# A new cost table for a kernel's instruction planner, with 36 instead of 100 products of zeros, in an attention block's forward and backward pass

## The chip, the cores and the metric

One core of a Trainium2 chip runs the whole program. Its engines work at the same time, each through its own list in order: PE multiplies matrices, DVE, ACT and POOL compute element by element, and SP's list here issues nearly all the DMA copies. The metric is the time of one execution in microseconds (us). A run of the profiler is one more execution; its span is what lies between its first and its last instruction.

## The reference

The block is a Branchformer layer on x of shape (2, 4000, 144): one branch is attention over all 4000 tokens, the other a gated unit with a convolution of five taps; both are merged by a second convolution and a matrix. What is computed is the output and, by `jax.vjp`, the gradients of x and of seven weights, in bfloat16.

```python
xa = _layernorm(x, axis=-1)
qkv = jnp.einsum('btd,de->bte', xa, w_qkv)
scores = jnp.einsum('btd,bsd->bts', q, k) * D ** (-0.5)
p = _softmax(scores, axis=-1)
attn = jnp.einsum('bts,bsd->btd', p, v)
glob = jnp.einsum('btd,de->bte', attn, w_att_out)
h = _gelu(jnp.einsum('btd,de->bte', xc, w_mlp_in))
...
loc = jnp.einsum('btd,de->bte', u * gc, w_mlp_out)
m = jnp.concatenate([glob, loc], axis=-1)
...
return x + jnp.einsum('btc,cd->btd', m, w_merge)
```
```python
_out, _vjp = jax.vjp(_f, x, w_qkv, w_att_out, w_mlp_in, dw_csgu, w_mlp_out, dw_merge, w_merge)
_grads = _vjp(grad_out)
```

## The kernel before

**Tiles.** A batch of 4000 tokens is 32 blocks of 125. The attention of one block of queries is one step; with two batches there are 64 steps, numbered through. In step s, four rounds of products fill PSUM tiles `ps` (L1276 with 128 rows, L1283 with the remaining 16): the scores of block s against 1000 keys, and beside them the gradient products of block s - 1. DVE copies the scores to `Pbuf` and takes their minimum (`S_min`, L1298), ACT makes the exponentials in place (L1304), and SP turns the two halves of `Pbuf` into `PT` by DMA transposes (L1308). PE then forms Y (`yz` from `PT`, L1325, 32 products in two halves). The gradient products go to `Sbuf` (ACT L1314 and DVE L1316, or DVE alone L1312), are transposed to `ST` (L1492) and give Z (L1363, 32 products). The products X (L1410) add the gradient of the keys' side; DVE sums them in `acc` (L1414, L1416). All Y and Z share one PSUM buffer of the pool `ps_yz`; X, `pt`, `pj`, `pd` and others share three of `ps_w`.

**Stages.** The head (steps 0 and 1) loads weights and tokens, normalises the tokens (statistics L380 and following, normalised blocks `xa_aug` by DVE L403, ACT L401 and POOL L405), transposes them (`pt`, L410 and L414), copies the result to `xaT_m` and `R` (L411, L415), and makes combined weights (`hps`) between the first scores. The first token tile is loaded by two copies, L42 (112 rows) and L43 (13 rows); so are the three others, and the gradient `go_q`. Beside the attention, in each batch, the gated branch runs in small units (`ph`, `pd`, `pc`, `pw`). At the change of batch (steps 26 to 38) the second batch's tokens and gradients (`xa_aug`, `pgo_h`, `gq`) are loaded, and the sums of the first are stored (`acc_d`). After step 63 a merge (`Hps`, `po`, `pm`, `pz`) and the weights' gradients end the program.

**Products of zeros.** The head also issues `WARM` products of a zero tile `wz` (L187), whose output `warm` is a tile of `ps_yz` that nobody reads.

**Order.** The program is first recorded in source order. `Planner.plan` then groups PE's products, works out which group needs which, and goes through modelled time: each engine, when free, takes the ready group with the smallest key. A key is the place in the source plus a number of `LEAD`, so a negative entry lets a kind of instruction go early and a positive one holds it back; zero products have the largest key, and fill gaps. An entry's name is stage, engine, output tile and size, for some tiles also which one of a step. No group may run further ahead than a window allows. `cost` gives an instruction's length and the time until its result can be used. The resulting order is fixed in each engine's list, whatever the true times are. Copies on SP's list also wait for the copy eight places ahead, since they use eight completion semaphores in turn.

Of the kernel before, what the change touches and what calls it, by code (L numbers as in the profile page):

```python
# [16 lines left out]
DR = 16  # L17
# [523 lines left out]
WARM = 100  # L541
# [247 lines left out]
class Planner:  # L789
# [101 lines left out]
    def cost(self, e, ins):  # L891
# [5 lines left out]
        if "Dma" in kind or "DMA" in kind:  # L897
            if kind == "InstDmaTransposeAnt":
                return (1.8, 4.3) if n > 1500 else (1.2, 3.0)
            return 0.5, 2.2  # L900
# [4 lines left out]
        f32 = any(a.bass_ap.tensor.dtype == F32 for a in aps_i[:1] + aps_o[:1])  # L905
        if e == "DVE":
            if kind in ("InstTensorTensor", "InstTensorCopy") and not psum and not f32:
                d = 0.155 + n / 1920.0
            elif kind == "InstTensorScalarPtr" and not psum and not f32 and len(aps_i) == 1:
                d = 0.22 + n / 3800.0  # L910
            elif kind == "InstBNStats":
                d = 0.3
            else:
                d = 0.155 + n / 960.0
            acc = len(aps_o) > 1
            if acc and n < 300:
                d += 0.14
            return d - 0.05 + (0.07 if acc else 0), d + (0.14 if acc else 0.06)
        if e == "Activation":
            d = 0.17 + n * (0.00096 if kind == "InstActivation" and not psum else 0.00084)  # L920
            return d - 0.08, d + 0.06
        d = {"InstTensorCopy": 0.24 + n / 1250.0, "InstTensorTensor": 0.16 + n / 480.0}.get(kind, 0.36 + n / 1700.0)
        if kind == "InstTensorTensor" and n <= 8:
            d = 0.43 + 0.15 * n
        return d, d + 0.06

    def plan(self, i0, i1, window=400, late=1 << 40, early=0):
# [111 lines left out]
        for a, b in self.pairs:  # L1039
            if a in gof and b in gof and gof[a] != gof[b]:  # L1040
                after[gof[a]].add(gof[b])

        for g in groups:
            d, end = 0.0, 0.0
            if g["e"] == "PE" and g["sg"]:
                m = [i for i in g["ins"] if i.ins[0].bass_ap.ap[0][1] >= 128]
                if len(m) < len(g["ins"]):
                    d = len(m) * 0.21 + 0.094 + 0.22 + 0.16
                    end = d - 0.14 + 0.22
# [3 lines left out]
            else:  # L1053
# [4 lines left out]
                if g["e"] == "PE":  # L1058
                    d, end = d + 0.02, end + 0.02
# [29 lines left out]
        for g, G in enumerate(groups):  # L1089
            if any(n.startswith("nm_") for _, n in allocs[g]):  # L1090
                turn = {}
# [1156 lines left out]
```

## Time and profile before

| what | us |
|---|---|
| median of 3 runs | 1287.58 (1287.13 to 1288.39) |
| the profiled execution | 1292.98 |
| its span | 1291.2 |
| PE busy in the span | 1257.1 |
| DVE busy | 1047.1 |
| ACT busy | 788.2 |
| POOL busy | 501.1 |
| mean granted clock of TensorE | 0.991 of full |

Busy time is the union of an engine's instructions. PE's products overlap each other, and the end of one is modelled, so PE can be shown as busy without a pause and yet stream fewer columns than it could. The matmul rows give the mean duration of one product (229 ns for 144 columns), not the spacing at which they follow each other (62 to 63 ns). 16 DMA engines moved 185.80 MB in 628829 packets, 604215 of them under 512 bytes; the queue of SP, ACT and the transposes (q1) took 76.7% of their time.

### The profile page before, as it was taken

Reading aid. Unit: us, or ns where it says so; the run is one execution under the profiler, and the core shown is the slowest. Engines: PE = TensorE matmul, PEld = TensorE weight load, DVE = VectorE, ACT = ScalarE, POOL = GpSimd, SP = SyncE. Lnnn points to the kernel's source line nnn. Section 1 sums busy time; section 2 is a strip of 40 time slices with the busy share of each in tenths; the row PEclk is TensorE's granted clock in tenths of the full one; section 3 lists DMA queues with packets and bytes.
Section 4 is the critical chain, followed back from the end, with each engine's and each line's share of the span. In section 5 each row is a group of like instructions: output and inputs, shape, how many; then the busy total and the mean of one; then the engine's idle time right before and its main releaser. Section 6 shows DMA issues by size and latency. Waiting matters only on the chain.

```text
span 1291.2 us, 39494 instructions
## 1 busy us (share of the span) xinstructions
PE 1257.1 (97%) x15974; PEld 1040.6 (81%) x15974; DVE 1047.1 (81%) x2809; ACT 788.2 (61%) x1291; POOL 501.1 (39%) x976
## 2 busy tenths in 40 slices
PE   8999999999999999899899999999999999899898
PEld 6578888888888887777678888888888888799897
DVE  6589888988888887898888888899889887666925
ACT  4776666666665666556656666667566665435561
POOL 6265335444443434232444434444443433132410
PEclk8899999999999999999999999999999999999999
DMA  4477888888888888889898898887778788959611
GB/s 126 94 141 136 155 144 152 143 145 150 137 151 142 145 143 162 158 145 174 168 155 148 133 149 135 151 137 146 137 142 154 136 155 167 188 123 208 186 44 50
DMA packets 628829, 185.80 MB, mean 144 GB/s; under 512 B 604215, under 2 KB 623065, under 8 KB 628625
## 3 DMA queue, kind: packets, MB, share of 16 engines
q1 hardware_dynamic: 627506, 181.88, 76.7%
q8 instruction: 125, 2.05, 0.6%
q0 software_dynamic: 592, 1.18, 0.3%
q14 instruction: 58, 0.48, 0.1%
q10 hardware_dynamic: 548, 0.21, 0.1%
HBM read 22.96 MB, written 16.69 MB: 31 GB/s over the span
## 4 chain that ended last, share of the span: by engine, by line
PE 83%; DMA 6%; DVE 3%; ACT 3%; SPq 2%; POOL 1%; issue 1%; ACTq 0%; POOLq 0%
PE X L1410 20%; PE ps L1276 15%; PE yz L1363 10%; PE yz L1325 9%; PE ps L1283 7%; DMA ST<-Sbuf 2%; PE po L1783 2%; DMA PT<-Pbuf 2%; PE pd L625 1%; PE pd L692 1%; PE pc L677 1%; PE pj L1249 1%; PE Hps L1698 1%; PE pt L1265 1%; PE pw L737 1%; DVE Pbuf L1298 1%
## 5 line engine op out<-in xcount | busy, mean ns | idle before, releaser
L1298 DVE TENSOR_SCALAR_CACHE_REDUCE Pbuf<-ps 125x1000 bf16<-125x1000 f32 x256 | 306.4, 1197 | 93.9 <-PE ps L1283 90.0
L1304 ACT ACTIVATE Pbuf<-Pbuf,nm 125x1000 bf16<-125x1000 bf16 x256 | 278.6, 1130 | 91.1 <-DVE nm L1300 90.7
L1410 PE MATMUL X<-QBs,Sbuf 125*125 125x144 bf16 x2048 | 298.8, 229 | 0.8 <-DVE acc L1414 0.4
L1410 PE MATMUL X<-QBs,Pbuf 125*125 125x144 bf16 x2048 | 292.3, 226 | 0.0
L1410 PEld LDWEIGHTS <-Sbuf 125*125 125x125 bf16 x2048 | 259.3, 137 | 26.0 <-issue 25.8
L1314 ACT CAST Sbuf<-ps 125x1000 bf16<-125x1000 f32 x190 | 188.7, 993 | 132.4 <-PE ps L1283 131.1
L1276 PE MATMUL ps<-xaT_m,qt 128*125 128x500 bf16 x1024 | 263.7, 378 | 2.9 <-DVE Pbuf L1298 2.1
L1410 PEld LDWEIGHTS <-Pbuf 125*125 125x125 bf16 x2048 | 260.6, 137 | 0.9 <-issue 0.9
L1416 DVE TENSOR_TENSOR acc<-X,acc 125x432 f32<-125x432 f32 (+1 forms) x373 | 200.5, 549 | 25.2 <-PE X L1410 22.3
L1363 PE MATMUL yz<-xa_aug,ST 125*125 125x144 bf16 x2048 | 150.6, 228 | 6.1 <-DMA ST<-Sbuf 4.8
L1276 PEld LDWEIGHTS <-qt 128*125 128x125 bf16 x1024 | 121.5, 137 | 42.8 <-issue 4.6
L1325 PE MATMUL yz<-xa_aug,PT 125*125 125x145 bf16 x2048 | 146.1, 228 | 6.5 <-DMA PT<-Pbuf 6.5
L1363 PEld LDWEIGHTS <-ST 125*125 125x125 bf16 x2048 | 139.4, 138 | 9.9 <-DMA ST<-Sbuf 6.1
L1325 PEld LDWEIGHTS <-PT 125*125 125x125 bf16 x2048 | 137.4, 137 | 9.6 <-DMA PT<-Pbuf 7.4
L1316 DVE TENSOR_TENSOR Sbuf<-Sbuf,Pbuf 125x1024 bf16<-125x1024 bf16 x190 | 134.6, 710 | 3.5 <-ACT Sbuf L1314 3.1
L1283 PEld LDWEIGHTS <-qt 16*125 16x125 bf16 x1024 | 36.6, 128 | 101.2 <-issue 101.2
L1283 PE MATMUL ps<-XR,qt 16*125 16x500 bf16 x1016 | 111.1, 420 | 0.0
L1343 POOL TENSOR_SCALAR QBs<-qb,rl 125x144 bf16<-125x144 bf16 x64 | 27.0, 422 | 180.5 <-DVE rl L1331 151.1
L1312 DVE TENSOR_TENSOR Sbuf<-ps,Pbuf 125x1000 bf16<-125x1000 f32 x66 | 78.8, 1194 | 6.7 <-PE ps L1283 6.2
L720 POOL TENSOR_TENSOR A_dwc<-l_fl,A_dwc 128x512 f32<-128x512 f32 (+2 forms) x48 | 37.0, 771 | 78.8 <-ACT l_fl L719 78.8
L1267 ACT COPY qt<-pt 128x500 bf16<-128x500 bf16 x62 | 35.9, 578 | 45.5 <-PE pt L1265 44.8
L595 POOL TENSOR_SCALAR l_a<-l_sq 125x576 bf16<-125x576 bf16 x32 | 22.5, 702 | 101.6 <-ACT l_sq L593 101.3
(576 smaller groups left out, 2411.3 us busy)
## 6 DMA issues: line engine op xcount, KB each, us to landing
Yn_d<-yn SPq DMA_DIRECT2D x64, 35.2 KB
Zn_d<-zn SPq DMA_DIRECT2D x64, 35.2 KB
ug_d<-ugr SPq DMA_DIRECT2D x32, 70.3 KB
PT<-Pbuf SPq DMA_TRANSPOSE x126
ST<-Sbuf SPq DMA_TRANSPOSE x126
Yg<-Yn_d SPq DMA_DIRECT2D x8, 252.0 KB
go_h<-in_grad_out_dram SPq DMA_DIRECT2D x8, 252.0 KB
Yg<-ug_d SPq DMA_DIRECT2D x8, 252.0 KB
```

The lines of the kernel that those rows point to most:

```text
L720: nc.gpsimd.tensor_tensor(acc, fl[0:rows, 0:n], acc, op=ALU.add)
L1276: mm = nc.tensor.matmul(pp[r // 2][:, r % 2, 0:CH], QT[i][:, 3 * h, :], bs(i)[0].xaT_m[:, c * CH:(c + 1) * CH], start=True, stop=False)
L1283: nc.tensor.matmul(pp[r // 2][:, r % 2, 0:CH], QT[i][rs, 1 + (q // 2 + h) % 2, :], xr, start=False, stop=True)
L1298: nc.vector.tensor_scalar(pv(Pbuf, i % NPB, c2), src, -1.0, 3.0e38, op0=ALU.mult, op1=ALU.min, accum_out=NM[i][:, c2:c2 + 1])
L1304: nc.scalar.activation(v, v, ACT.Exp, bias=NM[i][:, 4:5], scale=-1.0)
L1312: nc.vector.tensor_tensor(pv(Sbuf, i % NDB, c2), src, pv(Pbuf, i % NPB, c2), op=ALU.mult)
L1314: nc.scalar.copy(pv(Sbuf, i % NDB, c2), src)
L1316: nc.vector.tensor_tensor(sc, sc, pchunk(i % NPB, c2), op=ALU.mult)
L1325: nc.tensor.matmul(Y, PT[0:PB, j, 0:PB], S.xa_aug[:, j, 0:D + 1], start=(j == 0), stop=(j == NB - 1))
L1363: nc.tensor.matmul(Z, ST[0:PB, j, 0:PB], S.xa_aug[:, j, 0:D], start=(j == 0), stop=(j == NB - 1))
L1410: nc.tensor.matmul(X[:, jj, :], l, r, start=(n_ == 0), stop=(n_ == len(ops) - 1))
L1416: nc.vector.tensor_tensor(av, X[:, 0:nj, :], av, op=ALU.add)
```

## The change

The planner's model is altered in five ways, and its table of leads is new. The instructions that compute the result stay the same; their order in every list changes.

- `cost` has other lengths for DVE, ACT and POOL instructions, by kind, size and operands.
- DMA copies and transposes get a function `moved` and a model of the transfer queue: a transpose begins when the copies ahead have landed, and SP's list is held until then.
- The time from an instruction's end to its waiter depends on the waiter's engine (`wait`).
- `LEAD` has entries for two further stages, "B" (steps 26 to 38) and "E" (from step 60 on).
- `WARM` falls from 100 to 36, and a zero product may only be placed after the first group of `pt` has been (`lead`); its modelled length is doubled.

In the new order the first zero products stand behind the transposes of the first token tile, and the last four of them directly ahead of the first Y.

```diff
-WARM = 100
+WARM = 36
...
     LEAD = {
-        "H DVE raw 1008": -246, "H POOL ident 128": 38, "H POOL Wi 288": 113, "H POOL xa_aug 32": 32, "H POOL go_q 576": -13, "H SP go_q 576": -144,
...
+        "H SP go_q 1152": -233, "H SP go_q 288": -318, "H POOL qr 256": -26, "H DVE lnst 6": 16, "H DVE xa_aug 144": 105, "H ACT goT 250": 186,
...
+        "B SP pgo_h 288": -381, "B SP xa_aug 1152": 4, "B SP gq 576": -211, "B DVE pst 6": 72, "B SP acc_d 432": 145,
...
-                d = 0.155 + n / 960.0
-            acc = len(aps_o) > 1
...
+                d = 0.067 + n / 960.0
+            d += 0.06 * (one > 0) + 0.025 * (one > 1)
+            return d, d + 0.083
...
+    def moved(self, ins):
+
+        a = ins.outs[0]
+        n = self.count(a)
+        if type(ins).__name__ == "InstDmaTransposeAnt":
+            return (2 if n > 1500 else 3), n / 2048.0
+        b = n * (4.0 if a.bass_ap.tensor.dtype == F32 else 2.0) * a.bass_ap.ap[0][1]
+        src = next((q for q in ins.ins if hasattr(q, "bass_ap")), None)
+        far = src is not None and getattr(src.bass_ap.tensor, "tag_meta", None) is None
+        return (1 if far else 0), b / 200e3
...
+        lead = next(g for g, G in enumerate(groups) if G["e"] == "PE" and G["t"].startswith("pt"))
+        for g, G in enumerate(groups):
+            if G["x"] < 0:
+                after[g].add(lead)
...
-            c = "%s %s %s %d" % ("T" if G["x"] >= late else "H" if G["x"] < early else "A", E[G["e"]], t, 0 if G["e"] == "PE" else self.count(a))
+            c = "%s %s %s %d" % ("T" if G["x"] >= late else "H" if G["x"] < early else "B" if 26 <= step < 39 else "E" if step >= 60 else "A", E[G["e"]], t, 0 if G["e"] == "PE" else self.count(a))
...
+        wait = {"PE": 0.053, "DVE": 0.034, "Activation": 0.034, "Pool": 0.09, "SP": 0.055}
...
-                        if kind == "InstDmaTransposeAnt":
-                            n = 0.1 + n * 2.65 / 2000
...
-                        dmq = max(s + 0.2, dmq) + n
-                        end = max(s + G["d"], dmq + 2.1)
+                        how, v = self.moved(G["ins"][0])
+                        if how == 2:
+                            q = max(s + 1.83, dmq + 0.15)
+                            d, end = q - s + 0.05, q + 2.6
+                        elif how == 3:
+                            d, end = 1.25, max(s + 2.4 + 1.3 * v, dmq + 2.4 * v)
                         else:
-                            n *= (4.0 if a.bass_ap.tensor.dtype == F32 else 2.0) * a.bass_ap.ap[0][1] / 220e3
+                            end = max(s + (2.2 if how else 1.55) + v, dmq + v)
+                        dmq = max(dmq, end)
```

More of the change, by code (lines that the diff above doesn't have):

```diff
@@ L897, in cost @@
         if "Dma" in kind or "DMA" in kind:
-            if kind == "InstDmaTransposeAnt":
-                return (1.8, 4.3) if n > 1500 else (1.2, 3.0)
             return 0.5, 2.2
@@ L905, in cost @@
         f32 = any(a.bass_ap.tensor.dtype == F32 for a in aps_i[:1] + aps_o[:1])
+        one = sum(n > 8 and self.count(a) == 1 for a in aps_i[1:])
+        memset = "Memset" in kind or not aps_i
         if e == "DVE":
[L907 to L910, printed above, removed]
+            if memset:
+                d = 0.07 + n / (1000.0 if f32 else 2500.0)
+            elif kind == "InstTensorReduce":
+                d = 0.067 + n / 960.0
@@ L923, in cost @@
-        if kind == "InstTensorTensor" and n <= 8:
-            d = 0.43 + 0.15 * n
-        return d, d + 0.06
+                d = 0.21
+            elif n <= 8:
+                d = 0.08
+            elif kind in ("InstTensorTensor", "InstTensorCopy") and not f32 and (not psum or len(aps_i) == 1):
+                d = 0.067 + n / 1900.0
+                if psum and aps_o[0].bass_ap.ap[0][1] == DR:
+                    d += 0.12
+            elif kind == "InstTensorScalarPtr" and not psum and not f32:
+                d = 0.067 + n / 1920.0
+            else:
+                d = 0.067 + n / 960.0
@@ new lines, in cost @@
+            d += 0.06 * (one > 0) + 0.025 * (one > 1)
+            return d, d + 0.083
+        if e == "Activation":
+            d = 0.054 + n * 0.000821 + 0.09 * (one > 0) + 0.135 * (one > 1)
+            if not psum and one < 2 and kind == "InstActivation":
+                d += 0.046
+            return d, d + 0.108
+        if memset:
+            d = 0.04 + n / 1150.0
+        elif kind == "InstTensorCopy":
+            d = 0.105 + n / 1150.0
+        elif kind == "InstTensorTensor":
+            d = 0.43 + 0.15 * n if n <= 8 else 0.16 + n / 480.0
+        else:
+            d = 0.36 + n / 1700.0
@@ L1048, in plan @@
                     d = len(m) * 0.21 + 0.094 + 0.22 + 0.16
-                    end = d - 0.14 + 0.22
+                    end = d + 0.06
                 else:
@@ L1058, in plan @@
                 if g["e"] == "PE":
-                    d, end = d + 0.02, end + 0.02
+                    d += 0.023
+                    if g["x"] < 0:
+                        d *= 2.0
             g["d"], g["end"] = d, end
@@ L1087, in plan @@
         tagof = {n: t for al in allocs for t, n in al}
-        key, turn = [], {}
+        key, turn, step = [], {}, 0
         for g, G in enumerate(groups):
@@ L1091, in plan @@
                 turn = {}
+                step += 1
             a = G["ins"][0].outs[0]
             t = re.sub(r"\d*(_\d+)?$", "", a.bass_ap.tensor.name)
-            c = "%s %s %s %d" % ("T" if G["x"] >= late else "H" if G["x"] < early else "A", E[G["e"]], t, 0 if G["e"] == "PE" else self.count(a))
-            if c[0] == "A" and t in ("ps", "Pbuf", "Sbuf", "X", "acc", "yz", "PT", "ST"):
+            c = "%s %s %s %d" % ("T" if G["x"] >= late else "H" if G["x"] < early else "B" if 26 <= step < 39 else "E" if step >= 60 else "A", E[G["e"]], t, 0 if G["e"] == "PE" else self.count(a))
+            if c[0] in "ABE" and t in ("ps", "Pbuf", "Sbuf", "X", "acc", "yz", "PT", "ST"):
                 n = turn[c] = turn.get(c, -1) + 1
@@ L1168, in plan @@
                         left[t] -= 1
-                        lastuse[t] = max(lastuse[t], end + 0.055)
+                        lastuse[t] = max(lastuse[t], end + 0.053)
                         if not left[t] and t in live:
@@ L1175, in plan @@
                         same = groups[h]["e"] == e and e in ("PE", "DVE", "Activation", "Pool")
-                        ready[h] = max(ready[h], s if not data else (s + G["d"] + (0.0 if e == "PE" else 0.06)) if same else end + 0.055)
+                        ready[h] = max(ready[h], s if not data else s + d if same else end + wait[groups[h]["e"]])
                         heapq.heappush(ev, ready[h])
```

14 lines of the change are left out of this document (2 added, 12 removed), and 31 rows, old and new, of the table LEAD.

## The prediction

> **What bounds the kernel now.** I read the slices first, then busy time by stage, then PE's waits, then the order in time of the start.
>
> The slices of the page (PE, and the clock that TensorE was granted; a slice is 32.3 us):
>
> ```profile
> PE   8999999999999999899899999999999999899898
> PEclk8899999999999999999999999999999999999999
> ```
>
> PE is at 90% or more but for the start, a dip in the middle and the end, and only the first two slices lost clock. Busy time by stage (columns: stretch in us, then PE, PEld, DVE, ACT, POOL, clock, DMA):
>
> ```profile
> 340.00:440.00 100.00, 100.00 (x1281) 82.61 (x1280) 86.74 (x219) 65.84 (x109) 41.99 (x80) 1.00 0.83 146
> 440.00:540.00 100.00, 94.76 (x1202) 76.62 (x1200) 84.78 (x233) 56.98 (x83) 35.84 (x77) 1.00 0.84 152
> 540.00:640.00 100.00, 95.75 (x1180) 77.01 (x1181) 86.21 (x203) 59.53 (x83) 32.96 (x65) 1.00 0.90 162
> 640.00:740.00 100.00, 96.70 (x1188) 78.45 (x1188) 85.13 (x223) 63.99 (x102) 43.71 (x85) 0.98 0.86 149
> 740.00:840.00 100.00, 100.00 (x1273) 82.06 (x1271) 85.63 (x215) 64.62 (x103) 40.38 (x77) 1.00 0.84 142
> 1040.00:1140.00 100.00, 95.62 (x1234) 79.16 (x1233) 72.86 (x164) 52.65 (x73) 25.16 (x51) 1.00 0.88 166
> ```
>
> The steady steps (140 to 440, 740 to 1040) have no idle PE: there is nothing to win by a new order, only to lose. At the change of batch PE idles 5.24 + 4.25 + 3.30 = 12.8 us, and at the last steps 4.4. The clock by stretches that begin and end where it changed, and PE's waits from 440 to 740:
>
> ```profile
> 5.45:22.52 17.07, 13.78 (x136) 11.49 (x135) 13.90 (x70) 9.94 (x30) 11.57 (x20) 1.00 0.64 192
> 22.52:43.00 20.48, 20.48 (x115) 12.19 (x114) 10.47 (x23) 10.00 (x24) 11.74 (x34) 0.50 0.07 15
> 643.74:647.15 3.41, 3.41 (x20) 2.35 (x18) 1.16 (x6) 1.15 (x3) 1.23 (x3) 0.50 0.79 147
> ```
> ```profile
> PE yz L1325 <- DMA PT<-Pbuf: 4.8, 4, 2.5
> PE yz L1363 <- DMA ST<-Sbuf: 3.3, 3, 1.8
> PE ps L1276 <- DVE Pbuf L1298: 1.6, 2, 1.3
> ```
>
> So the start runs 20.48 us at half clock with PE never idle, and the change of batch waits above all for the DMA transposes (8.1 us). The start itself, PE's order and, last, DVE's and SP's first rows:
>
> ```profile
> 10.52 6.07 PE L187 MATMUL warm<-wz 128*128 128x256 bf16 x54
> 16.43 1.09 PE L410 MATMUL pt<-ident,xa_aug 125*128 125x125 bf16 x8
> 20.10 0.28 PE L1432 MATMUL pj<-RW,R 128*125 128x144 bf16 x1 [2.14 <-DVE R L415]
> 23.06 1.04 PE L1276 MATMUL ps<-xaT_m,qt 128*125 128x500 bf16 x2
> ```
> ```profile
> 6.38 1.78 DVE L380 BATCH_NORM_STATS2 lnst<-x_tp 125x6 f32<-125x144 bf16 x8 [2.71 <-DMA x_tp<-in_x_dram]
> ```
> ```profile
> 4.50 0.43 SPq L43 DMA_DIRECT2D x_tp<-in_x_dram  x1
> 10.25 0.31 SPq L42 DMA_DIRECT2D go_q<-in_grad_out_dram  x1
> ```
>
> The first tokens are complete 1.9 us after their last 13 rows were issued (4.50 to 6.38). PE then lacks work from 17.95 to 20.10 and for 0.96 us more, and after this the clock falls.
>
> **The sum** is made against the profiled execution: 1292.98 us, of which 1291.2 are its span. The median of the runs shown is 1287.58, 5.4 less, and I carry the difference over unchanged.
>
> **The zero products (100 to 36).** All 100 stand before 16.6 us, where PE has nothing else, so the 64 that go give no time back. The 36 that stay come after the first token transposes: in the new order 8 beside the first projections, 28 among the head's products up to the first Y. One takes 0.213 us at half clock (the first ones of this trace start 0.213 apart), 0.107 to 0.11 at full. They cost 2.9 us if the last 26 run at full clock and nothing is hidden, and nothing where PE would have waited for ACT. One thing more: their output holds the only buffer of ps_yz, so the first Y and Z (48 products at 63 ns, 3.0 us) can't run until the 36 are out. In the order before, they fill gaps at 49.97, 56.63 and 62.81; in the new order they stand behind three full quads of ps. That work is postponed, not saved.
>
> **The token loads.** In SP's new order the last 13 rows of the first token tile (L43) are 18th, not 7th: nine go_q copies (4 x 252.0 + 69.8 + 4 x 29.2 KB, 1.2 MB) stand before them. Each copy waits for the one eight places ahead. At some 0.41 us an issue the 18th goes out at 7.7; the same places were issued at 10.25 and 10.61 before, after a wait of 1.6. Landing takes 1.9 (row above) to 4.8 (a go_q copy of 139.5 KB, issued 5.42, let SP go on at 10.25). So 9.6 to 15.4; I take 12.5 against 6.38. Behind it on DVE: the statistics of all four tiles now stand before the first normalised block. One tile takes 2.4 us (6.38 to 8.77), four 9.6; then two small operations and four L403 of 0.3: first transposes at 23.5 (20.5 to 26.5), 7 us later than 16.43. What follows is ready sooner: tiles 2 to 4 are normalised by then, where before they came at 21.8, 25.3 and 29.0.
>
> **The head to the third full quad of ps**, which ended at 68.64 before. In the new order six more L403 stand before the first copy of R, and at half clock 32 transposes take 3.4 us (eight: 0.84, from 25.34 to 26.18), so the first ps comes 7.2 us after the first transposes: 30.7 against 23.06. From there PE has 24 us of products at full clock (counted from the order, each at its spacing in this trace: 0.21 us per 500 columns, 63 ns per 144), plus 2.9 of zeros, plus 2.7 if the clock stays at half until 36: 60.4 without waits. ACT is the other chain: busy some 35 us from 17.55 to 68.64, less 2.5 for instructions that moved across these ends, from 25.3 on: 58. It idled 3.75 of 25.64 us from 43.0 to 68.64, and I add such waits: 64. That is 4.6 us early with 3.0 us of work still owed, and with the later stages' small waits I call the **head 0**, bounds -5 (clock up at once) to +6 (loads at 15.4 and half clock until 50).
>
> The clock decides here, so its rows: it changed at 5.45, 22.52 and 43.00, steps of 3.41 us apart (5 and 6 of them). Counting the columns that matmuls stream (transposes included), it rose after windows filled to 1.00, 1.01 and 0.95 and not after 0.72 to 0.92; it fell after 0.29 and 0.21, not after 0.43. In the new order the two windows from 23.5 fill to 0.87 and 0.7, the third (two quads of ps) to about 1.0. Hence 36, with an uncertainty of a window.
>
> **The change of batch (steps 26 to 38), which get leads of their own.** I laid PE's products between the last ps of a step and the Y or Z that needs its transposes, at this trace's spacings. Before, the mean cover is 19.0 us for Y's first half, 20.5 for its second, 17.3 and 14.4 for Z's; after, 21.2, 23.3, 19.3 and 15.9. The waits were at most 2.5 us. SP's copies there are not fewer (17 instead of 15 between the first two PT), but the token loads are spread over three transposes more. I let the 1.5 to 2.8 us of cover take two thirds of the 8.1 us, 5.4, and with them the empty window (0.94 us busy of 3.42 at 640.32) and its half-clock one (3.41 / 2 = 1.7): **-7**, bounds -12 (all idle) to +1 (waits moved on).
>
> **The last steps.** Of 4.4 us idle, 3.2 are waits for PT and ST. Before, 16 copies for the merge (Yg, VUl, VUsl) stand between SP's last transposes, in the new order 6, the others behind them; the covers shrink by 2 to 5 us to what the steady steps have. **-2**, bounds -4 to +3. The merge after 1140 keeps its products, other copies: 0, bounds -3 to +3.
>
> **The steady steps.** Covers by the same count are 13.2, 16.8, 12.2 and 8.2 us at least, before 13.6, 17.4, 13.3 and 8.0, where PE did not wait. DVE (86% busy) has the same instructions. **+1**, bounds 0 to +15 (rival below).
>
> Sum: 0 - 7 - 2 + 1 = -8. Span 1283.2, run 1285.0, median **1279.6**.
>
> **Rivals.** *The clock rises at once.* The Trainium skill, "TensorE: Matmul & The Clock Gate" (Part 1, the HAM clock gate), says that one busy window of about 3.4 us lifts the clock to full. In rows: full clock from 27 instead of 36 us saves up to 9 / 2 = 4.5 us of PE time, of which ACT's chain may eat some: head -4, total -12, **1275.6**. Against it: 22.52 to 43.00, six windows with PE busy 100% in the profile and the clock at 0.50. That speaks for counting columns rather than busy time, and so does the rise at 43.00.
>
> *The stalls only move.* The block of 17 copies still stands before a PT, at 0.45 us each 7.7 us of SP. Then the change of batch gives 0 and the rest -1: **1286.6**, no change. For it: SP's copies are all still there. Against: longer covers.
>
> *The steady steps pick up a wait: slower.* Place: ps behind DVE's S_min (L1298), DVE being 86% busy and having waited only 21.5 us for PE in 300. 276 rows of L1276 at 16 a step make 17.4 us a step, some 48 steps outside the change of batch. From 0.19 us a step on, the other stages' gain of 9 is gone; at 0.25 it is +12, in all +3: **1290.6**. For it: every instruction was reordered and PE has no slack there. Against: the covers and DVE's list are alike.
>
> **How the numbers follow.** Forecast 0.46 (1279.6, own range 1274 to 1285), clock at once 0.15, stalls move 0.14, steady wait 0.25 (a late head beyond my bound counted with it). No change is within 0.2%, 2.6 us. Faster: 0.45 + 0.15 + 0.02 = 0.62; same 0.13; slower 0.25. The range, 1268 to 1293: below, the head's and the batch's bounds together; above, the steady wait at 0.3 us a step.
>
> **What would show it.** Right: first transposes near 23.5, clock 0.50 until 33 to 38 and then 1.00 throughout, PE idle from 440 to 740 under 8 us with the two DMA waits under 4, steady stretches at 100.00. Wrong: transposes before 19; half clock past 45; PE idle in a steady stretch; waits for PT and ST that stay at 8 us.

## The result, and the profile after

| | before | changed |
|---|---|---|
| median of five runs beside each other | 1288.17 us (1287.13 to 1290.83) | 1304.37 us (1301.82 to 1305.5) |
| profiled execution | 1292.98 us, span 1291.2 | 1304.79 us, span 1303.0 |

The ratio is 1.012, with an interval of 1.0103 to 1.0136: the change makes the kernel slower by some 16 us. The forecast was 1279.6 with a range up to 1293; the time lies outside it, on the other side of no change. The slower rival had the right place. (Beside the experiments below the kernel before takes 1284.5 to 1301.1 us, longer the lower its mean granted clock, which goes from 0.997 to 0.984, and the changed kernel takes 1301.8 to 1306.0 at 0.997 to 1.000 in all its runs, so a ratio moves by some tenths of a per cent with the runs that it is taken from.)

In the changed kernel the attention's lines stand 32 further down: ps is L1308 (128 rows) and L1315 (16 rows), S_min L1330, Y L1357, Z L1395, X L1442, acc L1448. First the slices, PE and the granted clock:

```profile
PE   3999999999999999999999999999999999999998
PEclk9999999999999999999999999999999999999999
```

Every slice of the clock shows 9 and PE's dip in the middle is gone; only PE's first slice is worse (3 instead of 8). The 9s say less than they seem to: the clock's record begins with its rise at 27.60, although five zero products at 25.36 still last 1.27 us, as at half clock, and the two windows of 3.41 us at half clock from 655.65 and 1119.86 are too short to change a digit. A slice shows tenths, so what was lost must be smaller than a tenth and spread out. The stretches show it (columns: stretch, then PE, PEld, DVE, ACT, POOL, clock, DMA):

```profile
340.00:440.00 100.00, 98.16 (x1235) 80.18 (x1233) 85.02 (x222) 63.23 (x102) 43.46 (x83) 1.00 0.87 144
440.00:540.00 100.00, 97.50 (x1236) 79.29 (x1235) 87.54 (x230) 61.71 (x89) 37.48 (x76) 1.00 0.81 148
540.00:640.00 100.00, 96.22 (x1184) 77.24 (x1180) 90.21 (x212) 60.12 (x82) 32.39 (x66) 1.00 0.91 165
640.00:740.00 100.00, 96.82 (x1208) 79.24 (x1207) 84.74 (x210) 62.85 (x103) 43.51 (x82) 0.98 0.83 148
740.00:840.00 100.00, 98.75 (x1233) 80.04 (x1232) 88.63 (x231) 61.57 (x99) 40.52 (x79) 1.00 0.85 146
1040.00:1140.00 100.00, 96.94 (x1191) 77.61 (x1190) 78.15 (x179) 57.11 (x80) 24.24 (x54) 0.98 0.90 161
```

The two steady stretches, 340 to 440 and 740 to 840, had 100.00 and now have 98.16 and 98.75. The change of batch gained 2.74, 0.47 and 0.12. PE's waits over the whole run (us in total, times, longest):

```profile
PE pt L410 <- ACT xa_aug L401: 10.0, 1, 10.0
PE ps L1308 <- DVE Pbuf L1330: 8.4, 24, 0.7
PE pt L410 <- DVE xa_aug L403: 5.0, 1, 5.0
...
PE yz L1357 <- DMA PT<-Pbuf: 2.9, 2, 2.0
PE yz L1395 <- DMA ST<-Sbuf: 2.8, 1, 2.8
PE yz L1395 <- ACT ty L1373: 2.2, 4, 1.1
```

The waits for the DMA transposes fell from 6.5 and 4.8 us to 2.9 and 2.8, as the forecast wanted. In their place ps waits 24 times, never longer than 0.7 us, for the PSUM buffer that S_min reads; before it was 4 times, 2.1 us in all. 19 of the 24, 6.2 us, lie from 140 to 440 and from 740 to 1040, where the kernel before has none. The page's chain of work that ended last says the same by engine; the first line is of the kernel before:

```profile
PE 83%; DMA 6%; DVE 3%; ACT 3%; SPq 2%; POOL 1%; issue 1%; ACTq 0%; POOLq 0%
```
```profile
PE 61%; DVE 23%; DMA 5%; issue 4%; ACT 3%; POOL 2%; SPq 1%; DVEq 0%; ACTq 0%; POOLq 0%
```

DVE is no busier (81% of the span both times, 1047.1 and 1058.3 us), but it now lies on the chain for 23% of it instead of 3%.

Where the time went can be added up. PE's own products, without zeros, need 1196.6 us at full clock in every kernel of this study (each at its spacing in the trace). The table gives, for each stretch, its length less the products that PE started in it: idle PE, half clock and zeros together. A row adds up to the span less 1196.6.

| us lost in | 0-140 | 140-440 | 440-740 | 740-1040 | 1040-1140 | rest | sum |
|---|---|---|---|---|---|---|---|
| before | 41.2 | 4.0 | 21.3 | 4.1 | 6.8 | 17.2 | 94.6 |
| changed | 44.8 | 11.2 | 18.0 | 10.5 | 6.5 | 15.4 | 106.4 |
| difference | +3.6 | +7.2 | -3.3 | +6.4 | -0.3 | -1.8 | +11.8 |

The steady steps lose 13.6 us, more than the 11.8 in all; the rest nearly cancels out. Where in a step they are lost can be read from the same spacings, because a pause before a product shows as a longer spacing, also where it is too short for the list of waits. A quad is four products of L1308 and the four of L1315 behind them. Summed over the two steady stretches, the pauses directly in front of the quads of ps are 0.1 us in the kernel before and 11.0 in the changed one, 10.9 of the 13.6. Nearly all of the 11.0 stands in front of 29 quads, and each of these starts within 0.1 us behind the end of an S_min. (The profiled execution of the kernel before ran 4.8 us above its median, that of the changed one at its median; hence 11.8 here and 16 between medians.)

One of the 24 waits, row by row. PE's order in time in the changed kernel (start, duration, engine, line; in brackets the idle time that the profile puts down to a releaser):

```profile
236.22 1.01 PE L1308 MATMUL ps<-xaT_m,qt 128*125 128x500 bf16 x4
237.16 0.43 PE L1315 MATMUL ps<-XR,qt 16*125 16x500 bf16 x4
...
239.20 0.23 PE L1442 MATMUL X<-QBs,Pbuf 125*125 125x144 bf16 x1
239.69 1.01 PE L1308 MATMUL ps<-xaT_m,qt 128*125 128x500 bf16 x4 [0.26 <-DVE Pbuf L1330]
```

and DVE in the same stretch:

```profile
235.57 0.16 DVE L1363 RECIPROCAL rl<-yz 125x1 f32<-125x1 f32 x1
235.76 0.37 DVE L1366 SCALAR_TENSOR_TENSOR dj<-yz,rl,qb 125x144 bf16<-125x144 f32 x1
236.05 0.08 DVE L1366 DVE_READ_ACCUMULATOR dj<-yz,rl,qb 125x1 f32 x1
236.17 0.21 DVE L1368 SCALAR_TENSOR_TENSOR nd<-delta,rl 125x1 f32<-125x1 f32 x1
236.30 0.35 DVE L708 SCALAR_TENSOR_TENSOR l_dd<-pd,rsr,l_w 125x144 bf16<-125x144 f32 x1
236.58 0.59 DVE L1448 TENSOR_TENSOR acc<-X,acc 125x432 f32<-125x432 f32 x1
237.42 0.37 DVE L708 SCALAR_TENSOR_TENSOR l_dd<-pd,rsr,l_w 125x144 bf16<-125x144 f32 x1 [0.25 <-POOL l_w L702]
237.82 0.69 DVE L709 TENSOR_TENSOR dhr<-l_dd,gpr 125x576 bf16<-125x576 bf16 x1
238.44 1.19 DVE L1330 TENSOR_SCALAR_CACHE_REDUCE Pbuf<-ps 125x1000 bf16<-125x1000 f32 x1
```

The quad of ps ended at 237.59. S_min could have begun then and begins at 238.44, because DVE is still at its list; it ends at 239.63. The next ps, due at 239.27 by the spacing of the products, starts at 239.69. Now look at the list. rl ends at 235.73 and dj, which reads it, starts at 235.76, 0.03 after the end. But l_dd (236.30) starts 0.08 before nd's end, and acc (236.58) 0.07 before l_dd's. An instruction that does not need its predecessor overlaps its end; one that does, does not. Over the changed kernel's trace the pairs rl-dj (63), mv-ve (32), l_dd-dhr (27), l_hg-st (18) all begin 0.034 to 0.036 us after the end, and independent neighbours 0.076 to 0.085 before it: **a dependant right behind costs DVE 0.117 us more**. The new planner has no such term: for two instructions of one engine it takes the moment when the engine is free (`s + d`), where the old one added 0.06 us and had longer lengths. So it sets them back to back. The list of the change's parts ahead of the prediction lacks this line of the diff:

```diff
-                        ready[h] = max(ready[h], s if not data else (s + G["d"] + (0.0 if e == "PE" else 0.06)) if same else end + 0.055)
+                        ready[h] = max(ready[h], s if not data else s + d if same else end + wait[groups[h]["e"]])
```

In the kernel before, the same three instructions:

```profile
229.50 0.17 DVE L1331 RECIPROCAL rl<-yz 125x1 f32<-125x1 f32 x1 [0.19 <-PE yz L1325]
229.58 0.29 DVE L696 SCALAR_TENSOR_TENSOR l_gc<-pd,gd 125x144 bf16<-125x144 f32 x1
229.79 0.09 DVE L696 DVE_READ_ACCUMULATOR l_gc<-pd,gd 125x1 f32 x1
229.79 0.36 DVE L1334 SCALAR_TENSOR_TENSOR dj<-yz,rl,qb 125x144 bf16<-125x144 f32 x1
...
230.51 0.15 DVE L1336 SCALAR_TENSOR_TENSOR nd<-delta,rl 125x1 f32<-125x1 f32 x1
```

l_gc stands between rl and dj, and another l_gc and two small operations between dj and nd: nothing stalls. (In the wait above, three such stalls are 0.35 us of S_min's 0.85; another 0.25 is l_dd's wait for POOL.) Between 100 and 1140 us the traces have 34 such stalled pairs before and 295 after, 4 and 35 us of DVE. S_min begins on average 0.24 us after the end of its quad before and 0.38 after. And from 100 to 440 and 740 to 1040, 2% of the S_min have a product of ps starting within 0.1 us behind their end before, 25% after: among the latter are the quads in which PE waited.

### The profile page after: what moved, and what is told of

It is laid out like the page before. It is cut to its first block, busy times and chain, and to the rows that moved or that the text cites. A ratio compares the mean times of both kernels' runs of the same rounds, so it can differ in the third digit from the quotient of the medians.

```text
span 1303.0 us, 39331 instructions
## 1 busy us (share of the span) xinstructions
PE 1250.8 (96%) x15910; PEld 1032.9 (79%) x15910; DVE 1058.3 (81%) x2809; ACT 786.8 (60%) x1291; POOL 501.8 (39%) x976
## 4 chain that ended last, share of the span: by engine, by line
PE 61%; DVE 23%; DMA 5%; issue 4%; ACT 3%; POOL 2%; SPq 1%; DVEq 0%; ACTq 0%; POOLq 0%
PE X L1442 14%; PE ps L1308 11%; PE yz L1357 7%; PE yz L1395 7%; DVE Pbuf L1330 6%; PE ps L1315 5%; DVE acc L1448 3%; PE po L1815 3%; DVE Sbuf L1348 2%; PE Hps L1730 2%; DVE Sbuf L1344 1%; ACT Pbuf L1336 1%; DMA PT<-Pbuf 1%; PE pw L737 1%; DMA acc<-acc_d 1%
## 5 line engine op out<-in xcount | busy, mean ns | idle before, releaser
L1330 DVE TENSOR_SCALAR_CACHE_REDUCE Pbuf<-ps 125x1000 bf16<-125x1000 f32 x256 | 305.8, 1195 | 78.2 <-PE ps L1315 77.9
L1336 ACT ACTIVATE Pbuf<-Pbuf,nm 125x1000 bf16<-125x1000 bf16 x256 | 275.4, 1127 | 80.3 <-DVE nm L1332 79.9
L1442 PE MATMUL X<-QBs,Sbuf 125*125 125x144 bf16 x2048 | 296.5, 228 | 1.9 <-DVE acc L1448 0.8
L1442 PE MATMUL X<-QBs,Pbuf 125*125 125x144 bf16 x2048 | 292.3, 226 | 0.5 <-POOL QBs L1379 0.4
L1442 PEld LDWEIGHTS <-Sbuf 125*125 125x125 bf16 x2048 | 259.6, 137 | 17.0 <-issue 16.3
L1308 PE MATMUL ps<-xaT_m,qt 128*125 128x500 bf16 x1024 | 262.7, 376 | 9.5 <-DVE Pbuf L1330 8.4
L1442 PEld LDWEIGHTS <-Pbuf 125*125 125x125 bf16 x2048 | 260.6, 137 | 2.1 <-issue 1.7
L1448 DVE TENSOR_TENSOR acc<-X,acc 125x432 f32<-125x432 f32 (+1 forms) x373 | 198.5, 548 | 19.4 <-PE X L1442 16.8
L1308 PEld LDWEIGHTS <-qt 128*125 128x125 bf16 x1024 | 123.9, 136 | 53.3 <-issue 15.0
L1395 PE MATMUL yz<-xa_aug,ST 125*125 125x144 bf16 x2048 | 148.2, 228 | 5.1 <-DMA ST<-Sbuf 2.8
L1357 PE MATMUL yz<-xa_aug,PT 125*125 125x145 bf16 x2048 | 147.4, 228 | 3.3 <-DMA PT<-Pbuf 2.9
L1395 PEld LDWEIGHTS <-ST 125*125 125x125 bf16 x2048 | 137.8, 138 | 12.2 <-issue 8.8
L1357 PEld LDWEIGHTS <-PT 125*125 125x125 bf16 x2048 | 138.4, 137 | 6.7 <-DMA PT<-Pbuf 3.7
L1315 PEld LDWEIGHTS <-qt 16*125 16x125 bf16 x1024 | 36.3, 128 | 99.7 <-issue 99.7
L1315 PE MATMUL ps<-XR,qt 16*125 16x500 bf16 x1016 | 111.3, 422 | 0.0
L1377 POOL TENSOR_SCALAR g<-qb,rl 125x144 f32<-125x144 bf16 x64 | 26.7, 417 | 105.0 <-DVE rl L1363 104.5
L1291 POOL COPY qr<-qb 125x64 bf16<-125x64 bf16 x124 | 35.0, 313 | 57.9 <-ACT qb L1283 57.7
```

The lines of the kernel that those rows point to most:

```text
L1308: mm = nc.tensor.matmul(pp[r // 2][:, r % 2, 0:CH], QT[i][:, 3 * h, :], bs(i)[0].xaT_m[:, c * CH:(c + 1) * CH], start=True, stop=False)
L1315: nc.tensor.matmul(pp[r // 2][:, r % 2, 0:CH], QT[i][rs, 1 + (q // 2 + h) % 2, :], xr, start=False, stop=True)
L1330: nc.vector.tensor_scalar(pv(Pbuf, i % NPB, c2), src, -1.0, 3.0e38, op0=ALU.mult, op1=ALU.min, accum_out=NM[i][:, c2:c2 + 1])
L1336: nc.scalar.activation(v, v, ACT.Exp, bias=NM[i][:, 4:5], scale=-1.0)
L1357: nc.tensor.matmul(Y, PT[0:PB, j, 0:PB], S.xa_aug[:, j, 0:D + 1], start=(j == 0), stop=(j == NB - 1))
L1395: nc.tensor.matmul(Z, ST[0:PB, j, 0:PB], S.xa_aug[:, j, 0:D], start=(j == 0), stop=(j == NB - 1))
```

## The experiments

The theory, then, is this: the new plan lets DVE's dependants stand back to back, each costs 0.117 us that the plan doesn't have, and since the plan is tight S_min hands the delay to ps. The other explanation: the new leads crowd the quads of ps, whatever DVE does. The kernel before ran beside each group of runs, with medians of 1291.4 to 1294.5 us, so ratios to it are compared. Columns from the third on are us lost by stretch, as above; the last three are stalled pairs between 100 and 1140 us, the share of S_min with a product of ps within 0.1 us behind their end ("tight"), and the pauses in front of the quads of ps in the two steady stretches, in us.

| run | ratio (interval) | 0-140 | 140-440 | 440-740 | 740-1040 | 1040-1140 | rest | pairs | tight | ps |
|---|---|---|---|---|---|---|---|---|---|---|
| before | 1 | 41.2 | 4.0 | 21.3 | 4.1 | 6.8 | 17.2 | 34 | 2% | 0.1 |
| changed | 1.012 (1.0103-1.0136) | 44.8 | 11.2 | 18.0 | 10.5 | 6.5 | 15.4 | 295 | 25% | 11.0 |
| e9_after | 1.0096 (1.0059-1.0132) | 45.9 | 10.8 | 17.8 | 10.5 | 6.9 | 15.7 | 295 | 25% | 10.9 |
| e1_sep | 1.0074 (1.005-1.0097) | 45.4 | 8.2 | 17.1 | 8.6 | 6.7 | 15.5 | 203 | 19% | 6.3 |
| e2_dep | 1.0131 (1.0092-1.0169) | 45.5 | 10.6 | 25.0 | 8.1 | 4.6 | 17.3 | 72 | 15% | 4.3 |
| e3_oldleads | 1.0438 (1.0396-1.0479) | 43.6 | 21.8 | 28.9 | 18.0 | 2.5 | 34.7 | 356 | 17% | 6.9 |
| e4_warm | 1.0141 (1.01-1.0182) | 50.8 | 11.1 | 17.4 | 10.0 | 4.4 | 18.8 | 296 | 25% | 10.9 |
| e5_adj | 1.0046 (1.0025-1.0067) | 42.2 | 4.6 | 23.4 | 5.4 | 5.8 | 17.9 | 323 | 7% | 0.5 |
| e6_hold | 0.9962 (0.9943-0.998) | 35.1 | 3.8 | 21.6 | 4.0 | 9.1 | 17.6 | 35 | 1% | 0.1 |
| e7_tuned | 1.0014 (0.999-1.0037) | 40.2 | 6.5 | 18.1 | 5.5 | 4.5 | 18.6 | 73 | 11% | 2.5 |
| e8_tuned | 1.0044 (1.002-1.0069) | 42.5 | 7.5 | 17.4 | 7.2 | 7.2 | 17.0 | 66 | 15% | 4.5 |
| e10_reserve | 1.0039 (1.0018-1.006) | 39.3 | 6.0 | 26.9 | 7.4 | 6.1 | 16.3 | 65 | 3% | 1.6 |
| e11_hold | 0.9962 (0.9938-0.9987) | 35.0 | 4.0 | 20.9 | 4.0 | 8.5 | 16.0 | – | 1% | 0.1 |

The changed kernel's repetition (e9_after) gives its stages again within 1.1 us, and those of the steady steps within 0.4; that is the noise to read the table with. The e-runs were made on several occasions, and the changed kernel has 1304.37 and 1304.57 us at the median on two of them.

**e9_after**, the changed kernel unchanged. The ratio, 1.0096, lies just under the range expected; the kernel before is slower beside it, the changed one is not faster.

> The changed kernel once more, beside e7_tuned and e8_tuned on the same chip: 1.010 to 1.014 of the kernel before's time, as at first; its profile tells how much of the stages' figures is repeated from run to run (within 1 us a stage expected).

**e1_sep: the pairs alone taken apart.** Behind the finished plan, on DVE:

```diff
+        D, k_ = order["DVE"], 0
+        while k_ + 2 < len(D):
+            a, b = D[k_], D[k_ + 1]
+            if a in preds[b] and not groups[a]["ins"][0].outs[0].bass_ap.tensor.name.startswith(("acc", "xa_aug", "Pbuf", "Sbuf")):
+                for m_ in range(k_ + 2, min(k_ + 5, len(D))):
+                    c = D[m_]
+                    if not allocs[c] and groups[c]["d"] <= 0.75 and ready[c] <= times[b] and not any(x_ in preds[c] for x_ in D[k_ + 1:m_]):
+                        D.insert(k_ + 1, D.pop(m_))
+                        break
+            k_ += 1
```

> The changed kernel with its plan as it is; behind the plan, on DVE alone, 157 instructions that need nothing of their neighbours are moved one to three places forward, between an instruction and the next one that reads its result. PE's, ACT's, POOL's and SP's orders are untouched. Theory (DVE's dependants stand back to back, each holds DVE 0.117 us longer than planned, and S_min comes late for the next ps): 157 x 0.117 = 18.4 us of DVE stall go, PE's waits for ps behind S_min (8.4 us in the profile after) fall to about 5, the steady stretches 140 to 440 and 740 to 1040 win 2 to 3 us each, and the time falls 4 to 8 us below the changed kernel's. Rival (the new leads bunch the quads of ps, and DVE's neighbours don't matter): the time stays within 2 us of the changed kernel's, with the waits for ps at 7.5 to 9.

The median is 1301.56 us, 2.8 to 3.0 below the changed kernel's, and the profiled span falls by 4.8 (1303.0 to 1298.2). As a time this is not clear of noise: the ratio's interval overlaps that of e9_after, and the fall is short of the 4 to 8 us expected. The stages are clearer: the two steady stretches win 3.0 and 1.9 us, the pairs fall by 92, and the pauses in front of ps fall from 11.0 to 6.3 us. Its wait for ps:

```profile
PE ps L1318 <- DVE Pbuf L1340: 6.0, 13, 1.4
```

Fewer waits, as expected (8.4 us, 24 times, in the changed kernel). The leads, and the orders of PE, ACT, POOL and SP, are those of the changed kernel, so an explanation that leaves DVE's order out falls short. (The moves also change what stands in front of S_min; no run moves as many instructions elsewhere for comparison.)

**e5_adj: the pairs alone put into the kernel before.** Behind its plan, a dependant is moved up behind what it reads:

```diff
...
+                for m_ in range(k_ + 2, min(k_ + 7, len(D))):
+                    b = D[m_]
+                    if a in preds[b]:
+                        if groups[b]["d"] < 0.7 and all(x_ not in preds[b] and x_ not in after[b] for x_ in D[k_ + 1:m_]) and a not in preds[D[k_ + 1]] and max([fin[p] for p in preds[b] if p != a], default=0.0) + 0.06 <= fin[a]:
+                            D.insert(k_ + 1, D.pop(m_))
+                        break
...
```

> The kernel before with its plan as it is; behind the plan, on DVE alone, an instruction that reads the result of another one up to six places ahead is moved up right behind it, where its other operands are ready by then. No other engine's order changes. Back-to-back dependants on DVE rise from some 30 to about 240, so 200 x 0.117 = 23 us of DVE stall are put in. Theory (such pairs hold up S_min and with it ps): waits for ps behind S_min rise from 2.1 us to 4 to 8, idle PE appears in the steady stretches that had none, and the kernel becomes 3 to 8 us slower. Rival (DVE, 86% busy, has room for them and the loss comes from the leads): within 2 us of the kernel before, steady stretches at 100.00 as they were.

Slower by 0.46%, 5.7 us between medians, as expected in time but not in place: the expected waits for ps did not come. The steady stretches, with more pairs (323) than the changed kernel has, lose only 0.6 and 1.3 us more than the kernel before:

```profile
140.00:240.00 100.00, 100.00 (x1285) 83.03 (x1284) 88.69 (x231) 65.96 (x106) 44.17 (x86) 1.00 0.87 149
240.00:340.00 100.00, 99.84 (x1264) 81.77 (x1263) 88.07 (x227) 64.47 (x104) 43.86 (x85) 1.00 0.82 145
```

PE stays at 100.00 and 99.84. So the pairs by themselves are not the 13.6 us. The old order leaves slack between most S_min and the quads behind them (2% are tight, 7% with the pairs put in) and swallows nearly all of it: the pauses in front of ps are 0.5 us. It takes both, then, the pairs and a plan that counts on the time they cost. Most of e5_adj's loss lies outside the steady stretches and is not explained here.

**e3_oldleads: the new planner with the old table of leads.**

> The new planner (lengths, waits, transfer queue, 36 zero products) with the leads of the kernel before, one table for all steps. Rival (the new leads bunch ps): the steady stretches are again without waits and the time is within 5 us of the kernel before's, 1283 to 1293. Theory (the planner puts DVE's dependants back to back whatever the leads): waits for ps as in the changed kernel or more, the steady stretches grow by 5 to 15 us each over the kernel before's, and the time is 1298 to 1315.

Far slower than expected by either, 4.4%, and worst of all runs in the steady steps. The other explanation falls: it doesn't take the new leads. Leads are fitted to a planner, and the old table under the new arithmetic gives still more waits, ps among them:

```profile
PE yz L1396 <- ACT ty L1374: 13.7, 18, 3.4
PE ps L1309 <- DVE Pbuf L1331: 11.8, 22, 1.7
```

**e2_dep: the missing wait put into the new planner.**

```diff
-                        ready[h] = max(ready[h], s if not data else s + d if same else end + wait[groups[h]["e"]])
+                        ready[h] = max(ready[h], s if not data else s + d if same and e == "PE" else end + wait[groups[h]["e"]])
```

> The changed kernel, planned again with one rule of the planner changed: on DVE, ACT and POOL an instruction that reads the one before it counts as ready at that one's end plus the wait, instead of at the moment when the engine is free. Leads, lengths, transfer queue and zero products stay. Theory (the missing wait of dependants is the cause): pairs of DVE instructions that stand back to back and depend on each other fall from about 190 to under 40, waits for ps behind S_min to under 4 us, and the time falls 8 to 16 us below the changed kernel's, to 1288 to 1296. Rival (leads that bunch ps): the same waits remain, the time falls by less than 4 us.

A miss in time. The pairs fell to 72, S_min's mean delay to 0.22 us, below that of the kernel before, and the pauses in front of ps from 11.0 to 4.3, as the theory has it; but the median is 1310.5 us, 6 above the changed kernel's:

```profile
PE yz L1357 <- DMA PT<-Pbuf: 5.6, 5, 2.9
PE yz L1395 <- ACT ty L1373: 5.5, 7, 1.9
...
PE ps L1308 <- DVE Pbuf L1330: 3.6, 7, 1.3
```

What ps no longer waits for DVE, Y waits for PT and Z for ty; the change of batch loses 25.0 instead of 18.0. The planner's own end (the modelled time at which its plan ends) went from 1252.2 to 1268.3 us: it now sees the cost but, with leads fitted to the other rule, does not avoid it.

**e7_tuned and e8_tuned: the rule of e2_dep, and leads fitted to it.** The leads were changed at random and kept when the plan's own end fell.

> The planner of run e2_dep (dependants on one engine wait) with a lead table fitted to that rule: 416 leads, changed at random and kept where the plan's own end fell, from 1268.3 to 1248.0; nothing else differs. Theory (the leads of the changed kernel were fitted to a plan in which dependants cost nothing, and e2 was slow because its table no longer fitted): back-to-back dependants stay under 100, the steady stretches grow no more than 1 to 4 us over the kernel before's, and the time is below the changed kernel's by 14 to 22 us, at 0.990 to 1.000 of the kernel before's. The plan ends 34 to 39 us before the chip in the changed kernel and in e2_dep, hence 1282 to 1287. Rival (the plan's arithmetic misses something larger than the dependants): no more than 6 us below the changed kernel.

> As e7_tuned, with a second table found from another random start (428 leads, plan's end 1248.7). The same expectations; the two runs show how far the chip's time depends on the table when the plan's end is the same: within 5 us of each other if the plan says nearly all, further apart if stalls that the plan doesn't know decide.

e7_tuned is level with the kernel before, 9.5 us under the changed kernel that ran beside it (1295.05 against 1304.57). That is less than the 14 to 22 expected and more than the rival's 6. Its steady stretches lose 6.5 and 5.5 us, so 4.7 and 5.0 of the 7.2 and 6.4 that the changed kernel lost more than the kernel before are back. (No run has leads fitted again without the rule, so what the search alone would win isn't known.) The wait for ps is down to the level of the kernel before:

```profile
PE ps L1352 <- DVE Pbuf L1374: 1.9, 5, 0.7
```

e8_tuned, whose plan ends within 0.7 us of e7_tuned's, takes 4.6 us longer on the chip; 2.7 of that is in the steady steps. So a plan's end, even with the rule put right, says the time to some 5 us and no better: the profiled span is 41.9 us longer than the plan in e7_tuned and 46.6 in e8_tuned (and 50.8 in the changed kernel, not the 34 to 39 of the expectation). Of the 3.9 us that e7_tuned still loses there, 2.4 still stand in front of ps, behind an S_min.

**e10_reserve: a buffer of ps counts as free 0.2 us later**, and leads fitted again.

```diff
-                        lastuse[t] = max(lastuse[t], end + 0.053)
+                        lastuse[t] = max(lastuse[t], end + (0.253 if t.startswith("ps_") else 0.053))
```

> The planner of e7_tuned with one more rule: a buffer of ps counts as free 0.2 us later than its reader's end, so that the plan keeps a reserve in front of every quad of ps; the lead table is fitted anew from that of e7_tuned (418 leads). The plan's own end is the same as e7_tuned's (1249.3 against 1248.0). Theory (what e7_tuned still loses in the steady steps is DVE's small delays that a plan without reserve hands straight to PE): quads that start within 0.1 us of their buffer's release fall from 10% to under 4%, the steady stretches lose 4 to 5 us each as in the kernel before instead of 6.5 and 5.5, and the time is 2 to 6 us below e7_tuned's, 0.994 to 0.999 of the kernel before's. Rival (the rest is lost elsewhere: DMA, clock): within 1.5 us of e7_tuned's 1.0014.

The reserve did what it should to the quads (3% tight, 1.6 us of pauses in front of ps), but the steady stretches lose 6.0 and 7.4 us all the same: the pauses in front of Y and Z grew there from 1.2 us in the kernel before to 4.8. What was won in front of ps was lost in front of Y and Z. The change of batch loses 26.9, and there, from 440 to 740, PE waits among others behind acc's reading of X:

```profile
PE pt L658 <- DVE acc L1490: 2.1, 1, 2.1
PE pj L1321 <- DVE acc L1490: 1.8, 1, 1.8
```

What causes the rest of the steady loss (2.5 and 1.4 us in e7_tuned) I leave open.

**e4_warm: the changed kernel with 100 zero products, not held.**

> The changed kernel with 100 zero products that aren't held and are planned at their own length, as before; leads and the rest of the planner are the new ones. Only the head is planned otherwise; the steady stretches keep their order. If the 36 held products cost what I gave them (2.9 us of PE, and Y and Z behind them), the time falls by 1 to 4 us and the clock changes at another place of the head; if they are hidden, it stays within 1.5 us of the changed kernel's. Under no theory does it win back more than 4 of the 16 us.

A miss with the opposite sign: the steady stretches are the same (11.1 and 10.0), the start loses 6.0 us more. The clock in its trace is full from 5.91, at half from 19.56 to 40.04, then full again; in the changed kernel it is full from 27.60 on and does not fall in the start. So in these profiled executions the held products had won 6 us; without them the changed start loses 9.6 more than the old one, with 20.48 us of half clock in both.

**e6_hold: the held zeros alone, in the kernel before.**

```diff
-WARM = 100
+WARM = 36
...
+        lead = next(g for g, G in enumerate(groups) if G["e"] == "PE" and G["t"].startswith("pt"))
+        for g, G in enumerate(groups):
+            if G["x"] < 0:
+                after[g].add(lead)
...
+                    if g["x"] < 0:
+                        d *= 2.0
```

> The kernel before with the zero products' part alone: 36 of them, held until the first token transposes and planned at twice their length. Its planner and its leads stay, so that from 140 us on the order is nearly the old one. By the run with 100 products in the changed kernel (head 6 us longer to 140 us, clock at half from 19.56 to 40.04) the held products fill PE's holes while the clock would fall: the clock rises once, before 30 us, and stays, and the time falls 3 to 8 us below the kernel before's. Rival (they only cost their own 2.9 us and delay Y and Z): the half clock of 20.48 us is still there and the time is 0 to 3 us above the kernel before's.

As expected, and it beats both kernels: 0.9962, in two runs on different occasions. The first 140 us win 6.1; 2.3 are given back from 1040 to 1140. PE in the start:

```profile
18.08 1.70 PE L187 MATMUL warm<-wz 128*128 128x256 bf16 x7
...
22.73 0.59 PE L1283 MATMUL ps<-xaT_m,qt 128*125 128x500 bf16 x2
23.25 0.63 PE L1290 MATMUL ps<-R,qt 16*125 16x500 bf16 x2
23.81 0.39 PE L187 MATMUL warm<-wz 128*128 128x256 bf16 x2
```

Seven zeros last 1.70 us before the clock rises at 21.94, and two last 0.39 after it. There are no zeros early, the clock rises once in the start, and ps finds it full. The 24 times of e6_hold and its repetition lie between 1284.1 and 1290.5 us, at a mean granted clock of 0.993 to 0.999; those of the kernel before beside them between 1284.5 and 1301.1, at 0.984 to 0.997. The held zeros do not lower the least time, then; they take away the half clock of the start. Number, hold and modelled length change together in e6_hold and e4_warm, so the runs do not tell which of them does it.

> The run e6_hold once more beside e10_reserve on the same chip: 0.994 to 0.998 of the kernel before's time. If e10_reserve's head and its change of batch gain as in e7_tuned and its steady steps as in the kernel before, the two come within 4 us of each other.

The repetition gives 0.9962 again, 11 us under e10_reserve. The stages of e10_reserve did not add up as that expectation put it.

## Why the prediction was wrong, point by point

**The steady steps: the step that failed.** They were put at +1, with the argument "the covers and DVE's list are alike". They cost 7.2 + 6.4 = 13.6 us, 0.40 for each of the 34 steps in those two stretches. This is the third rival with its place (ps behind S_min) and nearly its size (12, as 0.25 for each of 48 steps; the 0.25 was chosen, not read from a row, so the size is luck). The argument looked at which instructions DVE executes and how much PE work lies between ps and Y or Z. In their place the runs showed 11.0 us of pauses in front of ps, behind an S_min, where there had been 0.1. The cost came from what the diff showed and the working didn't use: the line in which a dependant of the same engine loses its 0.06 us. On an engine that is 86% busy, the same list in another order is not the same work. e1_sep shows that DVE's order alone moves the pauses in front of ps (11.0 to 6.3), e2_dep that the rule does (to 4.3), and e5_adj that back-to-back dependants without the tight plan do not (0.5); e7_tuned shows that with the rule and fitting leads 9.7 of the 13.6 come back.

**The change of batch: right mechanism, half the size.** -7 forecast, -3.3 measured. The waits for PT and ST from 440 to 740 fell from 8.1 to 2.9 us, by 5.2 where 5.4 were forecast. But Z's wait for ty rose from 0.3 to 2.2, and the half-clock window the gain was to include came back, at 655.65 for 3.41 us. That window is not what ate the gain: e9_after has none there and loses 17.8 instead of 18.0.

**The start: the events right, the sum wrong.** Statistics began at 12.65 (12.5 forecast), the second to eighth transposes at 23.76 (23.5), the first ps at 29.08 (30.7). One transpose came alone at 18.48, which the prediction had named as a sign of being wrong (before 19), as it had PE idle in a steady stretch. The profile's order in time:

```profile
18.48 0.29 PE L410 MATMUL pt<-ident,xa_aug 125*128 125x125 bf16 x1 [10.01 <-ACT xa_aug L401]
23.76 0.97 PE L410 MATMUL pt<-ident,xa_aug 125*128 125x125 bf16 x7 [4.99 <-DVE xa_aug L403]
```

The clock was full at 27.60, not 36: on this point the first rival was right, although its time was not. At 43 us the changed kernel was 1.1 us ahead (31.1 lost against 32.2). It lost 1.7 more than the kernel before from 43 to 80, and 3.0 more from 80 to 140, where the first full steps run. So most of the +3.6 is not the start but the steady loss again.

**The zero products.** The forecast ("the 64 that go give no time back", and a cost of 2.9 us for the others at most) was wrong in sign: in the profiled executions, holding 36 of them was worth 6 us of the start in both planners (e4_warm against the changed kernel, e6_hold against the kernel before), and 4.2 and 5.6 us between the medians of e6_hold, e11_hold and the kernel before beside them.

**The last steps and the merge**: -2 and 0 forecast, -0.3 and -1.8 measured. The sum is right, its two places are not: the gain came in the merge.

**The range.** Its upper end took a steady wait of 0.3 us a step, but subtracted a gain of 9 us elsewhere. That gain was 1.8 (3.6 - 3.3 - 0.3 - 1.8). The step from the profiled span to the median failed as well: 5.4 us between them were carried over, and the changed kernel's profile lies on its median.

## What to carry to other kernels

When a diff changes the arithmetic by which instructions are ordered, look for what the arithmetic leaves out, above all on the engine that feeds the bound one, and price what the new order will do with it: a length that is right and a wait that is missing make a tighter plan and a slower kernel. Count neighbours, not instructions: two lists with the same entries differ in how many dependants stand back to back. Separate the parts of a mixed change early; here one part was worth 5 us and lay hidden under one that cost more.

## What the runs showed of the hardware

- A DVE instruction that reads its predecessor's result starts 0.034 us after the predecessor's end, an independent one 0.076 to 0.085 before it, in the pairs named above (in the trace of the kernel before there are 16 rl-dj, one mv-ve and one l_hg-st, with the same 0.034 to 0.036). The Trainium skill, "VectorE: DVE Perf Modes" (The DRAIN you can't avoid), says that eight copies took as long with a semaphore after each as with one after the last, so that it cost nothing extra; in this trace, with short instructions of different kinds, the dependent order costs 0.117 us, and the measurement decides here.
- The clock had no one rule. In 3.41 us windows, as the share of the columns that could be streamed, it rose after one window at 0.91 (changed kernel, 27.60) and one at 0.88 (e6_hold, 21.94), but in e4_warm, where it had fallen at 19.56, not after 0.86 and 0.92; it rose at 40.04, after a window at 0.83 and six windows after its fall, like the kernel before (22.52 to 43.00). The prediction's reading, that it rises after windows filled to 0.95 or more, does not hold in these rows. The Trainium skill, "TensorE: Matmul & The Clock Gate" (Part 1, the HAM clock gate), says that one busy window lifts it: the first two agree, the other two don't.
